# PSUM readers in a fixed order, a score buffer that outlives the attention, and a new order list, in a planned transformer block

## The chip, the cores and the metric

One core of one Trainium2 chip. The metric is the device time of one execution, in microseconds; the time before is the median of three runs. Engine names are those of the profile: PE is the matmul engine (PEld its weight loads), DVE the vector engine, ACT the activation engine, POOL the general engine, SP the engine whose queue issues nearly all DMAs.

## The reference

One block over x of 1 x 2048 x 512, float32: adaptive layer norm from a condition c, an attention of 32 heads of 16 with a compressive memory over four segments of 512, then a dense layer pair (512 to 1792 to 512) with squared ReLU. Cut to its core:

```python
mod = silu(c) @ w_mod                      # six rows of 512: sa, ca, ga, sb, cb, gb
h = layernorm(x) * (1 + ca) + sa
q, k, v = h @ wq, h @ wk, h @ wv           # 32 heads, 4 segments
for s in range(4):
    logits = q_s @ k_s.T * scale + mask    # mask: -1e9 where the key comes after the query
    a_dot = softmax(logits) @ v_s
    a_mem = (phi(q_s) @ M) / (phi(q_s) @ z + 1e-6)      # phi(t) = t + 1 or exp(t)
    o_s = g * a_mem + (1 - g) * a_dot
    M, z = M + phi(k_s).T @ v_s, z + phi(k_s).sum()
x = x + ga * (o @ wo)
h = layernorm(x) * (1 + cb) + sb
x = x + gb * (relu(h @ w1 + b1) ** 2 @ w2 + b2)
```

## The kernel before

**The work.** Matmuls run on float32 split into a high part (rounded to the engine's short float32) and a low part, three products for one. The attention goes in 16 units, u = 0 to 15: four segments s of four column blocks cc of 128 (eight heads each). A unit has a projection to q and k (`qk`), whose two PSUM banks are read by ACT (high part), DVE (low part), and for the memory by ACT twice more (Exp and Relu). The four parts lie in a tile `sg`; twelve DMAs per unit (line 847) spread them into `ST`, a buffer of 12 slots with one row per head set. `a_quad` computes scores for the row maxima (PE line 902, DVE line 907), which go through a transpose and a small DMA into ST's last row (`mt`, line 975). `b_quad` computes the scores again (line 1071), ACT takes the exponential (line 1088) into tiles `pt`, POOL masks the diagonal (line 1075), PE multiplies by v (line 1130), and after both halves a transpose (`fin`, line 1165) and DVE normalize. `mem` reads and updates the memory. Output rows of the first three segments go to DRAM (`o_dram`) and come back (`ot`) with rows of x (`xw`) for the product with wo (`wo_tile`, lines 1226 to 1228); the last segment's stay in `X1L`. `ln2` norms and transposes (`blnq`), ACT and DVE each apply two of four affines into `h2raw`.

**The dense layers.** The first product is done by a seven-product scheme for 2 x 2 blocks: `make_w1` forms seven blocks of w1 in DRAM (`w1_dram`) during the attention; `h2_ops` forms four differences T1 to T4 on POOL (line 1321) and seven operands H2o, each a high part by ACT and a low part by DVE (lines 1335, 1337); `ffn1` runs seven products (line 1484) per pair of column blocks p, `ffn2` the second layer (lines 1548 to 1550). w1 blocks come back by `fetch_w1` (line 1434, 1.75 MB each), w2 by `load_w2` (lines 1442 to 1446).

**The plan.** Nothing is issued where the code calls for it. Each step is a node of `Plan`, made by `op(engine, duration, function, priority, after=..., get=..., put=...)`: `after` are the nodes it waits for, `get` takes a slot of a pool, `put` gives slots back when their last user has run. `Plan.run` plays all nodes with assumed durations and latencies, with one running node per engine, and `emit` then issues the program in the order of the starts. Where `ORDER` has a list for an engine, that engine takes its nodes strictly in that order; a number is the node's place in the order of creation, and 8-39 stands for 8, 9, up to 39. PE has 1,315 entries, ACT 945, DVE 897, POOL 342, SP 403. The waits of the chip follow from the tiles that the issued instructions touch, not from the plan's edges.

Pools that matter here: `bank` (8 PSUM banks), `P` (3 tiles of 8 KB per partition, for `pt` and early weights), `sg` (1 tile of 8 KB), `g` (16 tiles of 2 KB), `w1` (2), `rr` (4), `tt` (3).

**Memory.** `ST` lies in the attention's pool `sb`. `open_ffn` closes that pool and opens `sb2`, in whose memory the dense layers' tiles are made. Its node `N_FFN` waits for all nodes made before it, the whole attention. These wait for `N_FFN`: the T differences, operands H2o 2 to 6, the w1 and w2 loads, and the four wo tiles of the last segment.

```python
N_FFN = op("NIL", 0.0, open_ffn, -20.0, after=list(PL.nodes))
```

## Time and profile before

| | us |
|---|---|
| median of the runs before | 773.69 (770.69 to 774.9) |
| the profiled execution, its own time | 773.55 |
| its span (first to last recorded instruction) | 771.7 |
| PE busy in the span | 755.8 |
| DVE, ACT, POOL busy | 595.1, 441.8, 321.6 |

How to read it: a row of the timeline has start, length, engine, line, operation and tiles. A row of the waits reads "engine line <- releaser: us in total, times, longest us", idle time of the engine by what ended it. The chain of waits is the work that ended last, followed back from the end. An issue on SP's queue (SPq) is not the transfer; that lands later. The attention fills the span up to about 450 us, the dense layers the rest.

### The profile page before, as it was taken

Reading aid. Unit: us, or ns where it says so; the run is one execution under the profiler, and the core shown is the slowest. Engines: PE = TensorE matmul, PEld = TensorE weight load, DVE = VectorE, ACT = ScalarE, POOL = GpSimd, SP = SyncE. Lnnn points to the kernel's source line nnn. Section 1 sums busy time; section 2 is a strip of 40 time slices with the busy share of each in tenths; the row PEclk is TensorE's granted clock in tenths of the full one; section 3 lists DMA queues with packets and bytes.
Section 4 is the critical chain, followed back from the end, with each engine's and each line's share of the span. In section 5 each row is a group of like instructions: output and inputs, shape, how many; then the busy total and the mean of one; then the engine's idle time right before and its main releaser. Section 6 shows DMA issues by size and latency. Waiting matters only on the chain.

```text
span 771.7 us, 18017 instructions
## 1 busy us (share of the span) xinstructions
PE 755.8 (98%) x6649; PEld 598.6 (78%) x6649; DVE 595.1 (77%) x1591; ACT 441.8 (57%) x1001; POOL 321.6 (42%) x400
## 2 busy tenths in 40 slices
PE   9999999999999999998999999999999999999998
PEld 8986667666787667775666678989889899989886
DVE  5887797889799697888899798777875875576554
ACT  2669878799979987786856754654211321231110
POOL 5574776578968677474313362441010020000000
PEclk9999999999999999999999999999999999999999
DMA  8686773445645334537560084865435555544641
GB/s 271 215 264 168 207 238 97 142 133 154 186 156 146 78 92 141 160 96 207 179 190 29 10 293 146 283 229 187 178 118 183 192 203 193 190 144 170 232 164 55
DMA packets 59265, 129.65 MB, mean 168 GB/s; under 512 B 8613, under 2 KB 23977, under 8 KB 55594
## 3 DMA queue, kind: packets, MB, share of 16 engines
q1 hardware_dynamic: 59026, 128.37, 51.8%
q8 instruction: 53, 0.87, 0.5%
q14 instruction: 34, 0.28, 0.1%
q10 hardware_dynamic: 152, 0.13, 0.1%
HBM read 81.29 MB, written 20.19 MB: 131 GB/s over the span
## 4 chain that ended last, share of the span: by engine, by line
PE 79%; ACT 6%; DVE 5%; DMA 4%; SPq 2%; issue 2%; POOL 0%; ACTq 0%; DVEq 0%; POOLq 0%
PE bh L1484 17%; PE bqk L795 8%; PE bpf L1549 7%; PE bpf L1548 7%; PE bpf L1550 7%; PE bpv L1130 6%; PE bv L868 5%; PE bpb L1071 5%; PE ba L902 5%; ACT pt L1088 3%; PE bwarm L542 2%; PE bwop L1226 2%; DVE ba L907 2%; PE blnq L613 2%; SPq L847 1%
## 5 line engine op out<-in xcount | busy, mean ns | idle before, releaser
L907 DVE CUSTOM_DVE_ANT_0 ba<-ba,msk 128x384 f32<-128x384 f32 (+2 forms) x384 | 192.6, 531 | 32.5 <-PE ba L902 23.3
L1088 ACT ACTIVATE pt<-bpb 128x512 f32<-128x512 f32 x320 | 170.3, 613 | 19.8 <-PE bpb L1071 18.1
L1484 PEld LDWEIGHTS bh<-H2o,w 128*128 128x128 f32 x1176 | 154.7, 189 | 11.2 <-ACT p L1510 1.3
L1484 PE MATMUL bh<-H2o,w 128*128 128x256 f32 x1176 | 158.2, 282 | 0.6 <-ACT p L1510 0.6
L1075 POOL TENSOR_SCALAR_AFFINE_SELECT pt<-pt 128x512 f32<-128x512 f32 x128 | 79.3, 636 | 99.7 <-ACT pt L1088 64.4
L795 PE MATMUL bqk<-HT,WQK 64*128 64x512 f32 x720 | 103.0, 397 | 0.0
L1530 ACT CAST rr<-xx 128x512 fp32r<-128x512 f32 x56 | 34.6, 621 | 97.7 <-DVE xx L1520 55.2
L1071 PE MATMUL bpb<-ST 64*128 64x256 f32 (+2 forms) x512 | 81.0, 351 | 5.4 <-DVE mx L907 3.0
L1130 PE MATMUL bpv<-pt,VT 128*32 128x512 f32 (+3 forms) x1024 | 82.6, 448 | 0.5 <-DVE mx L907 0.5
L902 PE MATMUL ba<-ST 63*128 63x256 f32 (+2 forms) x512 | 77.5, 344 | 1.8 <-DMA ST<-pad 0.8
L795 PEld LDWEIGHTS bqk<-HT,WQK 64*128 64x128 f32 x720 | 66.9, 185 | 10.9 <-issue 1.0
L902 PEld LDWEIGHTS ba<-ST 63*128 63x128 f32 x512 | 48.8, 185 | 27.4 <-issue 5.6
L1071 PEld LDWEIGHTS bpb<-ST 64*128 64x128 f32 x512 | 51.3, 186 | 23.3 <-DVE mx L907 6.0
L1548 PE MATMUL bpf<-w,rr 128*128 128x512 f32 x160 | 63.5, 397 | 0.0
L1549 PE MATMUL bpf<-w,rr 128*128 128x512 f32 x160 | 63.0, 394 | 0.0
L1550 PE MATMUL bpf<-w,rr 128*128 128x512 f32 x160 | 62.5, 391 | 0.0
L1130 PEld LDWEIGHTS bpv<-pt,VT 128*32 128x32 f32 x1024 | 28.4, 111 | 35.6 <-issue 26.0
L907 DVE DVE_READ_ACCUMULATOR2_ANT mx<- 128x1 f32 x384 | 54.3, 141 | 0.0
L868 PE MATMUL bv<-WVO,HT 64*128 64x512 f32 x384 | 54.2, 396 | 0.0
L1532 DVE TENSOR_TENSOR rr<-xx,rr 128x512 fp32r<-128x512 f32 x56 | 40.2, 720 | 15.3 <-ACT rr L1530 15.3
L1510 ACT COPY p<-bh 128x256 f32<-128x256 f32 x28 | 10.4, 370 | 60.2 <-PE bh L1484 41.2
L1321 POOL TENSOR_TENSOR tt<-tt,h2raw 128x512 f32<-128x512 f32 x4 | 5.2, 1296 | 91.1 <-DVE H2o L1337 91.1
(171 smaller groups left out, 1466.9 us busy)
## 6 DMA issues: line engine op xcount, KB each, us to landing
w<-w1d SPq DMA_DIRECT2D x28, 1792.0 KB
ST<-sg SPq DMA_DIRECT2D x192, 128.0 KB
w1d<-X1L SPq DMA_DIRECT2D x21, 512.0 KB
xt<-in_A_x SPq DMA_DIRECT2D x16, 256.0 KB
wm<-in_w_mod SPq DMA_DIRECT2D x16, 256.0 KB
xw<-in_A_x SPq DMA_DIRECT2D x16, 256.0 KB
X1L<-in_B_w SPq DMA_DIRECT2D x7, 512.0 KB
wr<-in_B_w SPq DMA_DIRECT2D x14, 256.0 KB
```

What stands on the lines that cost most here:

```text
L795: nc.tensor.matmul(bank(banks[w]), W3(w, k, x, cols.start, cols.stop)[r], HT[r, y, k], start=turn == k == i == 0, stop=turn == 1 and k == ...
L868: nc.tensor.matmul(bank(banks[t]), HT[r, x, k, (t2 + t) * P:(t2 + t + 1) * P], WVO[r, k, y], start=turn == k == i == 0, stop=turn == 1 and ...
L902: nc.tensor.matmul(dst[:, c0:c0 + n], ST[b:b + 63, 0, sl, qt * P:(qt + 1) * P], ST[b:b + 63, 1, sl, :n], start=True, stop=True)
L907: nc.vector.tensor_tensor_reduce(i, i, msk[:, 512 - n:], scale=1.0, scalar=-3e38, op0=ALU.add, op1=ALU.max, accum_out=o)
L1071: nc.tensor.matmul(dst, ST[b:b + 64, 1, sl, kb * P:(kb + 1) * P], ST[b:b + 64, 0, sl, q0:512], start=True, stop=True)
L1075: nc.gpsimd.affine_select(out=ap, in_=ap, pattern=[[0, ap.shape[1]], [1, P]], compare_op=ALU.is_ge, fill=0.0, base=0, channel_multiplier=-1)
L1088: ns = [op("ACT", 0.49, lambda j=j: nc.scalar.activation(buf("PPP"[n], pt)[:, i + j], bank(keys[j]), AF.Exp, scale=0.25), pr[slot] + 0.01 ...
L1130: nc.tensor.matmul(bank(o)[32 * hq:32 * hq + 32, q0:q0 + src.shape[1]], v[:, a:a + 32], src, start=start, stop=stop, tile_position=(0, 32 ...
L1484: nc.tensor.matmul(pb(i), A[:, x, kk], B[:, y, kk], start=kk == j == 0, stop=kk == 1 and j == 2)
L1548: nc.tensor.matmul(q, rh, wh, start=(i == 0), stop=False)
L1549: nc.tensor.matmul(q, rh, wl, start=False, stop=False)
L1550: nc.tensor.matmul(q, rl, wh, start=False, stop=(i == NF - 1))
```

## The change

Five things.

1. Readers of one PSUM bank get an order as plan edges: Exp and Relu of a qk bank wait for DVE's low part (before: for ACT's high part only); in `ln_transposed` and `ln2`, DVE's half of the affine waits for ACT's half. The operations are the same.
2. `sg` tiles are taken from pool `P`, which has 4 slots instead of 3; the separate `sg` pool of 1 is gone.
3. `ST` moves out of `sb` into a pool of its own that stays open. In the dense layers its slots are used again: 1 to 3 for `rr` tiles (the fourth in `sb2`), 4 to 7 for `w1` slot 0, 8 to 11 and 0 for operands H2o 2 to 6.
4. `h2_ops` of the first segment is made before `N_FFN` and no longer waits for it: its T differences take tiles of pool `g`, its operands wait for the last readers of the ST slots (units 14 and 15). The first w1 load waits for unit 13's readers. Node numbers from the old `N_FFN` (2777) to the old place of these 18 nodes (2883) go up by 18: the wo tiles' first transpose 2781 becomes 2799, the first w1 load 2820 becomes 2838.
5. All five lists of `ORDER` are new up to the last layers. Of the lists, the parts that matter in what follows: SP's four wo loads (2623, 2627, 2631, 2635), unit 14's fills (2392 to 2403) and the `ot` and `xw` loads (2640, 2650, 2660); PE's entries from the last wo matmul of the first three segments (2754 to 2757) through the first products (2903 to 2909) and the transposes of X1L (before: 2811, 2781, 2791, 2801; after: 2809, 2819, 2829, 2799); POOL's T differences (after: 2777 to 2780).

```diff
     "PE": """
...
-2611 2599 2716 2751 2717 2770 2615-2617 2766 2754 2619 2755-2757 2811 2781 2791 2801 2814-2816 2794 2817 2795
-2784-2785 2796 2906 2903-2904 2786 2905 2908 2797 2787 2804-2806 2907 2909 3142 2807 3066 3138 2926 2928 2927 3064
...
+2583 2566 2570 2495 2588 2747 2711 2592 2596 2603 2593 2599 2606 2611 2714-2717 2751 2594 2615-2617 2754 2619
+2755-2757 2903 2906 2904 2809 2819 2905 2908 2812 2822 2813 2823-2824 2829 2814 2799 2825 2832 2907 2802-2803 2909
...
     "POOL": """
...
+2428 2366 2531 2354 2513 2361-2362 2760 2462 2455 2463 2552 2467 2478 2485 2490 2486 2777-2778 2579 2780 2587 2586
+2779 2591 2609 2602 2610 2614 2885 2840 2844 3132 2849 2853 2862 2858 2867 2876 3389 2871 2894 2880 2889 3646
...
     "SP": """
...
-2110-2111 2115 1982 1793 269 2269 1460 2272 2278 2270 2277 2273 2003 2271 2275 276 2279 2268 2276 2274 2400 2176 2394
-2393 279 1928 2399 2398 2197 2392 2401 2396 2631 2397 2402 2623 2635 2403 2627 2395 2640 2650 2321 2660 2300 2670 2524
-2516-2518 2063 2710 2522 2520 2680 2525 2690 2519 2527 2523 2720 2700 2526 2521 2424 2750 2730 2445 2740 2548 2569
...
+1982 2115 2278 2275 2277 2268 1460 2270 2272 1658 2269 2271 276 2279 2273 2276 2003 2274 2176 2197 2400 2395 1928 1793
+2631 2627 2635 2623 2394 2640 2403 2399 2392 2398 2393 2321 2650 279 2397 2660 2401-2402 2300 2063 2516 2527 2518 2521
+2396 2524 2680 2523 2525 2517 2670 2700 2720 2520 2519 2740 2522 2730 2424 2526 2690 2445 2710 2838 2548 2569 2750
+2796-2797 2839 2843 2828 2798 2818 2884 2808 2847 2856 2848 2852 2861 2865 2857 2866 2874 2901 2875 2879 2870 2883
...
@@ -432,6 +431,9 @@
     gb_dram = dram.tile([1, D], F32, name="gb_dram")
     st_all = const.tile([P, NT, 2], F32, name="st_all")
     small = ctx.enter_context(tc.tile_pool(name="small", bufs=2))
+    NSLOT = 12
+    ST = ctx.enter_context(tc.tile_pool(name="stp", bufs=1)).tile([P, 2, NSLOT, 512], F32R, name="ST")
+    STf = ST.bitcast(F32)
     ph1 = ExitStack()
     sb = ph1.enter_context(tc.tile_pool(name="sb", bufs=1))
     ps = ctx.enter_context(tc.tile_pool(name="ps", bufs=1, space=PSUM))
@@ -450,10 +452,7 @@
                                 fill=0.0, base=-DH, channel_multiplier=1)
-    NSLOT = 12
     NV = 6
-    ST = sb.tile([P, 2, NSLOT, 512], F32R, name="ST")
-    STf = ST.bitcast(F32)
     VT = [sb.tile([P, 4 * VROW + 16], F32, name=f"VT{i}") for i in range(NV)]
     MB = sb.tile([P, 4, VROW], F32, name="MB")
     nc.gpsimd.memset(MB, 0.0)
@@ -461,11 +460,12 @@
         nc.gpsimd.memset(v, 1.0)
-    POOLS = {"bank": 8, **BANKS, "xr": 4, "P": 3, "g": 16, "sg": 1,
+    POOLS = {"bank": 8, **BANKS, "xr": 4, "P": 4, "g": 16,
              "mx": 2, "mt": 1, "oT": 2, "mv": 2, "ac": 1, "#F": 4, "xx": 3, "rr": 4, "wr": 3,
              "w1": 2, "w2": 5, "p1": 1, "u2": 2, "u3": 1, "tt": 3, "wx": 1, "wy": 1}
     HOME, KEPT = dict.fromkeys(("oraw", "e", "phi0", "phi1", "pk", "am", "on", "xr"), "g"), {}
+    HOME["sg"] = "P"
     PL = Plan(POOLS, ORDER)
     def op(*args, get=(), **kw):
@@ -635,7 +635,8 @@
             af = [op("ACT", 1.38, lambda: ln_affine("av", buf(pool, f), bank(b), sc, bi), pr + 0.01, after=[n, *MODC[sc]], put=[b])]
         else:
             af = [op("ACT", 0.69, lambda: ln_affine("a", buf(pool, f), bank(b), sc, bi), pr + 0.01, after=[n, *MODC[sc]], put=[b]),
-                  op("DVE", 0.64, lambda: ln_affine("v", buf(pool, f), bank(b), sc, bi), pr + 0.01, after=[n, *MODC[sc]], put=[b])]
+                  None]
+            af[1] = op("DVE", 0.64, lambda: ln_affine("v", buf(pool, f), bank(b), sc, bi), pr + 0.01, after=[af[0]], put=[b])
         h = act(512, lambda: ln_split(dst(), t, TL[f], low)[0](), pr + 0.02, sbuf=True, after=[*af, *wait], put=[f])
         l = op(low, 1.24 if low == "POOL" else 0.6, lambda: ln_split(dst(), t, TL[f], low)[1](), pr + 0.03, after=[h], put=[f], lock=True)
         return [h, l]
@@ -833,10 +834,10 @@
             ev[w] = (hi, lo)
             if s > 0 if w == 0 else s < NS - 1:
                 e, f = ("e", u, w), (f"phi{w}", u)
-                x1_ = act(512, lambda b=b, e=e: nc.scalar.activation(buf("e", e), bank(b), AF.Exp), p2 + 0.001, after=[hi],
+                x1_ = act(512, lambda b=b, e=e: nc.scalar.activation(buf("e", e), bank(b), AF.Exp), p2 + 0.001, after=[lo],
                           get=[("e", e)], put=[b])
                 x2_ = act(512, lambda b=b, f=f, w=w: nc.scalar.activation(buf(f"phi{w}", f), bank(b), AF.Relu), p2 + 0.002,
-                          after=[hi], get=[(f"phi{w}", f)], put=[b])
+                          after=[lo], get=[(f"phi{w}", f)], put=[b])
                 m_ = op("POOL", 1.57, lambda e=e: nc.gpsimd.tensor_scalar(TL[e], TL[e], 1.0, None, op0=ALU.min), p2 + 0.002, after=[x1_])
                 PHN[u, w] = op("POOL", 1.23, lambda e=e, f=f: nc.gpsimd.tensor_tensor(TL[f], TL[f], TL[e], op=ALU.add), p2 + 0.003,
                                after=[m_, x2_], put=[e])
@@ -1209,6 +1210,12 @@
     def x1(g):
         return LT["X1"][g // 4][:, g % 4]
+    def rr_tile(k):
+        if k not in TL:
+            q = PL.slot[k]
+            TL[k] = ST[:, :, 1 + q, :] if q < 3 else FF["sb"].tile([P, 2, L], F32R, name="rr", tag="rr3")
+        return TL[k]
+
     WON = []
     def load_wo(k, pr, after):
@@ -1253,8 +1260,10 @@
         n = pe("F", 0.355, tr, pr, after=heads + [N_FFN] if last else [ld], get=[("#D", b), (pool, ot)], put=() if last else [o])
         def hi():
-            home = FF["sb"] if last else LT["op"]
-            TL[ot] = home.tile([P, 2, D], F32R, name="oT", tag=f"{pool}{PL.slot[ot]}")
+            if last:
+                rr_tile(ot)
+            else:
+                TL[ot] = LT["op"].tile([P, 2, D], F32R, name="oT", tag=f"oT{PL.slot[ot]}")
             nc.scalar.copy(TL[ot][:, 0], bank(b))
         h = act(512, hi, pr + 0.01, after=[n], put=[b])
         l = dve(512, lambda: nc.vector.tensor_tensor(TL[ot][:, 1], bank(b), TL[ot][:, 0].bitcast(F32), op=ALU.subtract), pr + 0.01,
@@ -1292,8 +1301,9 @@
             def both(k, affine=affine):
                 affine(k)
                 affine(k + 1)
-            RAW[s] += [op(e, c, lambda k=k, both=both: both(k), pr[t] + 0.01, after=[n, *MODC[CB], *RAWUSE[s - 1], N_LATE], put=[b])
-                       for e, c, k in (("ACT", 0.69, 0), ("DVE", 0.64, 2))]
+            for e, c, k in (("ACT", 0.69, 0), ("DVE", 0.64, 2)):
+                n = op(e, c, lambda k=k, both=both: both(k), pr[t] + 0.01, after=[n, *MODC[CB], *RAWUSE[s - 1], N_LATE], put=[b])
+                RAW[s].append(n)
@@ -1303,9 +1313,7 @@
     def operand(j):
         if j < 2:
             return LT["ops"][j]
-        if "opb" not in FF:
-            FF["opb"] = [FF["sb"].tile([P, 2, 2, HALF], F32R, name=f"H2o{i + 2}") for i in range(5)]
-        return FF["opb"][j - 2]
+        return ST[:, :, (8, 9, 10, 11, 0)[j - 2], :].rearrange("p h (k n) -> p h k n", k=2)
     def h2_ops(s, at):
@@ -1317,10 +1325,13 @@
             key = ("tt", s, name)
             def go():
-                TL[key] = FF["sb"].tile([P, 2, HALF], F32, name="tt", tag=f"tt{PL.slot[key]}")
+                if s:
+                    TL[key] = FF["sb"].tile([P, 2, HALF], F32, name="tt", tag=f"tt{PL.slot[key]}")
+                else:
+                    TL[key] = sb.tile(SHAPES["e"], F32, name="tt", tag=f"g{PL.slot[key]}").rearrange("p (k n) -> p k n", k=2)
                 nc.gpsimd.tensor_tensor(TL[key], blk[x](), blk[y](), op=ALU.subtract)
-            node[name] = op("POOL", 1.55, go, at[0] + 0.09 * k, after=[N_FFN, *RAW[s], *(node[q] for q in (x, y) if q in node)], get=[("tt", key)],
-                            put=[("tt", s, q) for q in (x, y) if q in node])
+            node[name] = op("POOL", 1.55, go, at[0] + 0.09 * k, after=[*RAW[s], *(node[q] for q in (x, y) if q in node), *([N_FFN] if s else [])],
+                            get=[("tt" if s else "g", key)], put=[("tt", s, q) for q in (x, y) if q in node])
             blk[name] = lambda: TL[key]
         t_of("T1", "B12", "B11", 0)
         t_of("T2", "B22", "T1", 1)
@@ -1331,7 +1342,7 @@
         for j, name in enumerate(BO):
             key = ("tt", s, name)
             put = [key] if name in node else []
-            wait = [N_LATE if j < 2 else N_FFN] + (OPUSE[s - 1, name] if s else [])
+            wait = OPUSE[s - 1, name] if s else [N_LATE] if j < 2 else [q for pp in range(4) for q in STU[4 * (NU - 1 if j == 6 else NU - 2) + pp]]
             h = act(512, lambda j=j, name=name: nc.scalar.copy(operand(j)[:, 0], blk[name]()), at[1 + j], sbuf=True,
                     after=[*([node[name]] if name in node else RAW[s]), *wait], put=put)
             l = op("DVE", 0.6, lambda j=j, name=name: nc.vector.tensor_tensor(operand(j)[:, 1], blk[name](), operand(j)[:, 0].bitcast(F32),
@@ -1340,6 +1351,7 @@
             if name not in node:
                 use += [h, l]
         RAWUSE[s] = use
+        return [q for name in BO if name not in node for q in OPN[s][name]]
     gb = lambda: buf("oraw", ("t", "gb"))
     for p in range(NF // 2):
@@ -1398,14 +1410,14 @@
         FF["gbb"] = sb2.tile([P, D], F32, name="gbb")
         FF["b2g"] = sb2.tile([P, D], F32, name="b2g")
-    N_FFN = op("NIL", 0.0, open_ffn, -20.0, after=list(PL.nodes))
+    z = e + K_FF
+    def us(t):
+        return z + t / 14.0
+    free_of = {n.seq for n in h2_ops(0, [us(-7 + 0.7 * j) for j in range(8)])}
+    N_FFN = op("NIL", 0.0, open_ffn, -20.0, after=[n for n in PL.nodes if n.seq not in free_of])
     del HOME["xr"]
-    z = e + K_FF
     n_gbb = sp(lambda: nc.sync.dma_start(FF["gbb"], gb_dram.to_broadcast([P, D])), z - 3, 1 << 18, after=[N_FFN])
     n_b1 = sp(lambda: nc.sync.dma_start(b1c, b1.rearrange("(f p) -> p f", p=P)), z - 2.8, 1 << 14, after=[N_FFN])
-    def us(t):
-        return z + t / 14.0
-
     NP = NF // 2
     STEP = 10.44
     W1N, W2N = {}, {}
@@ -1417,6 +1429,8 @@
     def w1slot(p, s):
         k = ("w1", p, s)
+        if PL.slot[k] == 0:
+            return ST[:, :, 4:8, :].rearrange("p h s n -> p h (s n)")[:, :, :7 * 2 * P].rearrange("p h (a k n) -> p h a k n", a=7, k=2)
         if k not in TL:
             TL[k] = FF["sb"].tile([P, 2, 7, 2, P], F32R, name="w1", tag=f"w1{PL.slot[k]}")
         return TL[k]
@@ -1431,7 +1445,11 @@
     def fetch_w1(p, s, t0):
         key = ("w1", p, s)
-        n = sp(lambda: nc.sync.dma_start(w1slot(p, s).bitcast(F32), w1_dram[p]), us(t0 - 12), 7 << 18, after=[N_FFN, *W1D[p]], get=[("w1", key)])
+        first = p == s == 0
+        n = sp(lambda: nc.sync.dma_start(w1slot(p, s).bitcast(F32), w1_dram[p]), us(t0 - 12), 7 << 18, get=[("w1", key)],
+               after=[*W1D[p], *([q for pp in range(4) for q in STU[4 * (NU - 3) + pp]] if first else [N_FFN])],
+               soft=() if first else [LT["w1"]])
+        LT["w1"] = n
         W1N[p, s] = dict.fromkeys(AO, [n])
     def load_w2(p, t0):
@@ -1453,7 +1471,6 @@
     for p in range(NP):
         fetch_w1(p, 0, STEP * p)
         load_w2(p, STEP * p)
-    h2_ops(0, [us(-7 + 0.7 * j) for j in range(8)])
     kb = ("b2b",)
     n = sp(lambda: nc.sync.dma_start(buf("xr", kb), bass.AP(tensor=b2.tensor, offset=b2.offset, ap=[[0, P], [1, D]])), z + 0.2, 1 << 18,
            get=[("xr", kb)], after=[X1N[4 * NS - 1]])
@@ -1507,7 +1524,7 @@
             return op("DVE", D_ + 0.06, lambda: nc.vector.scalar_tensor_tensor(dst(), pb(i), bias[j], other(), op0=ALU.add, op1=ALU.add),
                       us(t0 + t), after=[N[i], n_b1, *after], **kw)
         L_, R_ = [lambda i=i: X[i]()[:, :HALF] for i in (0, 1)], [lambda i=i: X[i]()[:, HALF:] for i in (0, 1)]
-        a1 = act(HALF, lambda: nc.scalar.copy(P1(), pb(1)), us(t0 + 0.9), after=[N[1]], get=[("p1", p1)], put=[K[1]])
+        a1 = act(HALF, lambda: nc.scalar.copy(P1(), pb(1)), us(t0 + 0.9), after=[N[1], N_FFN], get=[("p1", p1)], put=[K[1]])
         d2 = add(1.7, U2, 6, P1, [a1], get=[("u2", u2)], put=[K[6]])
         d3 = add_b(2.4, U3, 7, U2, 1, [d2], get=[("u3", u3)], put=[K[7]])
         d4 = add_b(4.4, U2, 5, U2, 0, [d2, d3], put=[K[5]])
@@ -1524,9 +1541,7 @@
                 n = act(512, lambda i=i: nc.scalar.activation(X[i](), X[i](), AF.Square), us(t0 + t), sbuf=True, after=[n])
             def rr_(i=i):
-                if rr[i] not in TL:
-                    TL[rr[i]] = FF["sb"].tile([P, 2, L], F32R, name="rr", tag=f"rr{PL.slot[rr[i]]}")
-                return TL[rr[i]]
+                return rr_tile(rr[i])
             h = act(512, lambda i=i, rr_=rr_: nc.scalar.copy(rr_()[:, 0], X[i]()), us(t0 + t + 0.7), sbuf=True, after=[n], get=[("rr", rr[i])],
                     put=[x_[i]])
             l = op("DVE", 0.6, lambda i=i, rr_=rr_: nc.vector.tensor_tensor(rr_()[:, 1], X[i](), rr_()[:, 0].bitcast(F32), op=ALU.subtract),
```

293 lines of the change are left out of this document (143 added, 150 removed), and 11 rows, old and new, of the table ORDER.

## The prediction

> **What bounds the kernel now.** First view: the head of the profile page, the busy time of the engines.
>
> ```profile
> span 771.7 us, 18017 instructions
> PE 755.8 (98%) x6649; PEld 598.6 (78%) x6649; DVE 595.1 (77%) x1591; ACT 441.8 (57%) x1001; POOL 321.6 (42%) x400
> ```
>
> PE is busy for 98% of the span; no other engine passes 78%. So the question is where the 771.7 - 755.8 = 15.9 us without a matmul lie. The second view, busy time by stage, answers it (columns: stretch, its length, then busy time and count of PE, PEld, DVE, ACT, POOL, then clock, DMA share, GB/s).
>
> ```profile
> 0.00:25.00 25.00, 23.10 (x182) 21.41 (x183) 13.98 (x30) 9.50 (x20) 10.91 (x31) 1.00 0.85 279
> 25.00:350.00 325.00, 318.86 (x3642) 230.71 (x3642) 274.02 (x882) 271.84 (x656) 233.76 (x287) 0.99 0.53 154
> 350.00:375.00 25.00, 22.83 (x239) 13.61 (x236) 21.48 (x65) 19.38 (x43) 8.67 (x14) 0.93 0.64 191
> 375.00:450.00 75.00, 75.00 (x628) 50.99 (x627) 65.11 (x187) 48.51 (x103) 23.05 (x34) 1.00 0.37 119
> 450.00:475.00 25.00, 23.80 (x143) 20.29 (x142) 22.18 (x38) 10.91 (x22) 11.47 (x10) 1.00 0.55 186
> 475.00:768.00 293.00, 292.25 (x1825) 261.62 (x1823) 197.68 (x393) 81.61 (x161) 33.77 (x27) 1.00 0.52 184
> 768.00:771.70 3.70, 0.00 (x0) 0.00 (x0) 0.62 (x1) 0.00 (x0) 0.00 (x0) 0.96 0.20 74
> ```
>
> The gaps: 1.9 us at the start and 3.7 at the end, which nothing in the diff touches; 6.1 in the attention up to 350; 2.2 between 350 and 375; none up to 450; 1.2 at the change to the dense layers; 0.75 in the dense layers' 293 us. The dense layers have nothing to give. What can be won lies in 25 to 475.
>
> A gap in this count is too small, though. The third view, the timeline of PE where the attention ends, shows why (columns: start, length, engine, line, operation, tiles; in brackets the idle time before it and what ended it).
>
> ```profile
> 451.20 0.49 PE L1252 MATMUL bwot<-ident,X1L 128*128 128x128 f32 x3
> 452.49 1.64 PE L1252 MATMUL bwot<-ident,X1L 128*128 128x128 f32 x13 [0.80 <-DVE X1L L1188]
> 454.20 0.40 PE L1227 MATMUL bwop<-WVO,oT 128*128 128x512 f32 x1
> 454.92 0.50 PE L1228 MATMUL bwop<-WVO,oT 128*128 128x512 f32 x1 [0.32 <-DVE oT L1260]
> 455.25 0.39 PE L1226 MATMUL bwop<-WVO,oT 128*128 128x512 f32 x1
> 455.48 0.40 PE L1227 MATMUL bwop<-WVO,oT 128*128 128x512 f32 x1
> ```
>
> Back to back, a matmul of 512 columns starts 455.48 - 455.25 = 0.23 us after the one before, but its row is 0.39 long. Each gap hides 0.16 us under the end of the row before it. By starts, the wait for X1L costs 452.49 - 451.20 less three steps of 0.113 (13 transposes in 1.64 with a last row of some 0.28) = 0.95 us, and the wait for oT 454.92 - 454.20 - 0.23 = 0.49.
>
> **The change part by part.** The counts of the order text first: PE's list holds 1,315 entries and 160 changes of array mode in both versions, so no work and no mode change is added or removed. What moves is waiting.
>
> *Part 1, the dense layers begin earlier.* ST outlives the attention, so the first w1 block (into ST slots 4 to 7, after unit 13), the seven H2o operands and the T subtractions no longer wait for open_ffn. In the new PE list three products (2903, 2906, 2904) stand between the last wo matmul (2757) and the first transpose of X1L, and two more after the second transpose; before, four transposes stood there at once.
>
> ```profile
> 442.45 0.33 SPq L1434 DMA_DIRECT2D w<-w1d  x1
> 449.36 2.53 POOL L1321 TENSOR_TENSOR tt<-h2raw 128x512 f32<-128x512 f32 x2 [4.12 <-DVE h2raw L1290]
> 451.04 1.39 DVE L1188 TENSOR_TENSOR X1L<-X1L,am 128x512 f32<-128x512 f32 x1
> 451.96 1.61 POOL L1321 TENSOR_TENSOR tt<-h2raw,tt 128x512 f32<-128x512 f32 x1
> 457.17 2.58 DVE L1337 TENSOR_TENSOR H2o<-tt,H2o 128x512 fp32r<-128x512 f32 x2
> 457.46 3.45 POOL L1443 TENSOR_TENSOR wr<-wr,gbb 128x512 f32<-128x512 f32 x2
> 459.68 1.78 DVE L1337 TENSOR_TENSOR H2o<-h2raw,H2o 128x512 fp32r<-128x512 f32 x1
> 460.85 2.25 PE L1484 MATMUL bh<-H2o,w 128*128 128x256 f32 x18
> 461.38 0.68 DVE L1337 TENSOR_TENSOR H2o<-tt,H2o 128x512 fp32r<-128x512 f32 x1
> ```
>
> Today the first product starts at 460.85, because T1 starts at 449.36 and the operands follow. Three products are 18 matmuls, 2.1 us by starts, and cover the 0.95 and most of the 0.49; the rest of the 475 window's idle time (0.1 here and there) I leave. Taken: -1.4 us; ends 0 (the operands come as late as the transposes do now) and -2.0 (all idle time of 450 to 475 by starts). If the operands are late, the cover is gone and PE stands before 2903 instead of before the transpose. The four T subtractions (2.53 + 1.61 + one more of 1.3) go between the last unit's selects on POOL; POOL is busy 23 of 75 us there, so they cost nothing unless a select meets one, 1.3 us at most, with three score groups queued on PE as cover.
>
> Beside that the H2o rows: one takes 0.68 alone and 1.78 at 459.68 while POOL's L1443 runs, as the X1L add at 451.04 takes 1.39 beside a T subtraction. If all seven, moved into the attention's tail, met POOL like that, DVE would need 7 x 1.1 = 7.7 us more of the 9.9 us it has idle in 375 to 450, so nothing on PE as long as they fall into idle time. The Trainium skill ("SBUF — State Buffer", Who interferes with whom) says that a DVE instruction with two SBUF inputs contends with a GpSimd instruction that reads SBUF; the row agrees, and by it this part of the change would be a loss on DVE and not a gain, by up to those 7.7 us.
>
> *Part 2, the order.* One stall in the trace is long and has a place. The chain of waits and the waits of PE and DVE show it.
>
> ```profile
> 356.89 2.95 DMA wo<-in_A_wo
> 358.85 1.09 SPq L1216 DMA_DIRECT2D wo<-in_A_wo  x2
> 359.86 0.79 DVE wo L1217
> 361.37 0.50 PE bpb L1071 x3
> PE bpb L1071 <- DVE mx L907: 3.0, 4, 2.1
> DVE wo L1217 <- DMA wo<-in_A_wo: 2.8, 2, 2.1
> L847 SPq DMA_DIRECT2D ST<-sg x192: 607/608/2007, 32.4 to 395.8; - x192
> 362.25 0.58 SPq L1241 DMA_DIRECT2D ot<-o_dram  x1
> 362.88 0.56 SPq L1242 DMA_DIRECT2D xw<-in_A_x  x1
> 366.27 1.41 SPq L975 DMA_DIRECT2D ST<-mt  x2
> ```
>
> SP issues a wo load at 356.89, it lands 2.95 us later, DVE stands 2.1 us before L1217 with the row maxima (L907) behind it, and PE stands 2.1 us before a score group. In the old SP list eight of unit 14's twelve fills (L847, 0.61 us of SP each) stand ahead of that load (2631); in the new one two do, and the four wo loads follow each other. Six fills less are 3.6 us, more than the 2.1 that the load was late. Taken: -2.0. The price is on the other side of the queue. All fills of unit 14's first half (2392 to 2394, 2398 to 2400) stood ahead of the wo loads; its last one (2393) now stands behind the four of them (1.09 for two), one pair of ot and xw loads (0.58 + 0.56) and two more fills: 2.2 + 1.1 + 1.2 = 4.5 us. PE hides that only if these scores come late enough in its list; taken at 0, ends -2.1 and +2.4.
>
> For all else that is rearranged between 25 and 450 no row of before can say what it brings. The nearest are the gaps left, 6.1 us visible up to 350, and the single stalls of 2.1. I take 0, ends -4 (two thirds of the visible gaps) and +4 (two stalls like 361.37).
>
> *Part 3, the readers.* Exp and Relu of a qk bank now follow DVE's subtraction of the low part, DVE's half of an affine follows ACT's. In the waits of ACT, DVE and PE:
>
> ```profile
> ACT e L836 <- DVE sg L831: 3.3, 6, 0.8
> DVE sg L831 <- ACT phi L838: 1.6, 4, 0.7
> DVE h2raw L1290 <- ACT h2raw L1288: 5.9, 5, 2.6
> ACT lnf L619 <- DVE lnf L621: 2.1, 1, 2.1
> PEld ba L902 <- ACT e L836: 1.6, 2, 1.1
> PE ba L902 <- ACT phi L838: 0.4, 1, 0.4
> ```
>
> These engines already wait for each other, 12.9 us in all, with no edge between them in the old plan: as these rows show, readers of one bank are put in sequence anyway, in the order in which the plan had them start. So the edges add no wait on the chip; they only let the order be chosen with it. What reached PE is 0.4 visible and 1.6 on the weight loads. Taken: -0.8; ends -2.0 and +1.0 (Exp always last makes phi later; phi is needed by L995 and L1020 alone). Beside this the eight-KB tiles are four of one pool instead of three and one: PE waits for a pt tile's exp in nothing over 0.4, so 0, ends -1 and +1.
>
> **Sum.** The profiled execution took 773.55 us, span and 1.85 around it, 0.14 under the median 773.69. 773.55 - 1.4 - 2.0 - 0.8 = 769.35; 769.3 us, 0.57% less. Differences under some 0.5%, 3.9 us, are about what a measurement of this kernel can't tell from no change; the bound is 769.8.
>
> **Rivals.**
> A. *Given back* (no change). The stalls above go, but PE meets the next late thing: the attention is bounded by DVE and ACT as much as by PE in places (274 and 272 of 325 us busy up to 350), and a group that starts 2 us earlier waits 2 us longer for its exp. Then only the transition stays: 773.55 - 1.4 = 772.2. For it: the 6.1 us are spread thin. Against it: 350 to 450 has idle time on both.
> B. *Unit 14 starved* (slower). SP's queue from 345 on: the first half's fills come 4.5 us later, and the second half's last one (2396) stands behind two more ot pairs, two mt stores (1.41 each) and four fills of unit 15, another 2.3 + 2.8 + 2.4 = 7.5 us; the scores of unit 14 wait, and behind them DVE, ACT and the wo products. PE then stands 4.5 to 12.0 us; against the 4.2 won elsewhere it decides from 4.2 on. With half of the 7.5: 769.35 + 4.5 + 3.75 = 777.6. Against it: PE is without a gap from 375 to 450, so work is queued there.
> C. *More room than the rows of PE show.* Hidden gaps of 0.16 each mean that a better order can win more than 15.9 - 5.6. With -4 in the attention and the far ends of parts 1 to 3 (-2.0, -2.1, -2.0, -1): 762.4. The Trainium skill ("Perfetto Trace Analysis", Identifying the Most-Contended Engine) holds matmul busy time to be no measure of how near PE is to its limit, and takes weight-load busy time. By it the attention (25 to 450: 295.3 of 425, 69%) is far from the dense layers (261.6 of 293, 89%) and at their share would need 331 us, an estimate from the stages' rows that would put the time at 680; the mode changes, the same 160 in both lists, and the short products speak against reading it so, and no run here shows it.
>
> **How the numbers follow.** Forecast (765.5 to 770.5): 0.44, of which 0.38 is under 769.8. A (770 to 775): 0.31, same. B (774 to 781): 0.13, of which 0.07 is over 777.5. C (758 to 765.5): 0.12, faster. So faster 0.50, same 0.43, slower 0.07; I move 0.04 from same to slower, since the whole list between 25 and 450 is new and may hold a stall with no row before: 0.50, 0.39, 0.11. The range 761.5 to 777.5 leaves out the far half of C and the upper half of B, with what was moved to it: 2 in 10 at most. The likeliest case's own range is 765.5 to 770.5.
>
> **What would show it.** Part 1: in the changed profile the first bh product (L1484's line) starts near 451, right behind the last wo matmul of the attention, instead of 460.85, before the transposes of X1L, and PE's gap with releaser X1L is gone. Part 2: no wait of PE for mx near 2 us between 350 and 375; DVE's wait for a wo load is 0; if B is right, PE or PEld waits for ST filled from sg there. Part 3: ACT's wait for sg grows or stays, and DVE's for phi is gone. The dense layers' rows stay at 293 us from 475 on. The prediction is wrong if PE's idle time in 25 to 350 differs from 6.1 us by more than 4, or if the transition shows PE standing for H2o.

## The result and the profile after

| | before | after |
|---|---|---|
| median, us (4 runs each) | 772.19 (770.51 to 774.90) | 762.53 (761.64 to 765.40) |
| ratio | | 0.9857, 95% interval 0.9821 to 0.9893 |
| profiled execution, us | 773.55 | 762.98 |
| its span, us | 771.7 | 761.3 |

The change makes the kernel 1.4% faster, where 0.57% was forecast. The engines' busy times and the stages of the changed kernel (columns as before):

```profile
PE 749.7 (98%) x6649; PEld 598.1 (79%) x6649; DVE 582.7 (77%) x1591; ACT 440.1 (58%) x1001; POOL 322.3 (42%) x400
```

```profile
25.00:350.00 325.00, 319.64 (x3646) 233.61 (x3644) 271.55 (x895) 271.23 (x658) 234.68 (x286) 0.99 0.53 149
350.00:375.00 25.00, 24.60 (x269) 15.11 (x266) 23.86 (x67) 21.93 (x46) 12.14 (x20) 1.00 0.79 239
450.00:475.00 25.00, 25.00 (x157) 22.18 (x156) 18.95 (x34) 12.02 (x23) 9.97 (x8) 1.00 0.59 220
475.00:757.50 282.50, 282.39 (x1764) 253.34 (x1762) 186.27 (x380) 74.81 (x149) 30.36 (x24) 1.00 0.50 179
```

PE's share is 98% again. The transition has lost its gaps (25.00 of 25, 23.80 before), and the last stage is 282.5 us long instead of 293. But by these rows almost nothing happened up to 350 us: PE idle 5.4 us instead of 6.1. That is misleading, because equal times are not equal work. A mark that stands for the same step in both kernels shows it: the transposes that close a unit's head outputs (bfin), 16 for each unit. PE's timeline of before, the rows of units 5, 8, 10, 11 and 12, then the last matmul:

```profile
209.59 0.66 PE L1165 MATMUL bfin<-ident,oraw 64*128 64x64 f32 x16
286.66 0.66 PE L1165 MATMUL bfin<-ident,oraw 64*128 64x64 f32 x16
337.75 0.66 PE L1165 MATMUL bfin<-ident,oraw 64*128 64x64 f32 x16
361.66 0.94 PE L1165 MATMUL bfin<-ident,oraw 64*128 64x64 f32 x14
383.71 0.66 PE L1165 MATMUL bfin<-ident,oraw 64*128 64x64 f32 x16
767.49 0.40 PE L1550 MATMUL bpf<-w,rr 128*128 128x512 f32 x1
```

The same of after:

```profile
209.12 0.66 PE L1166 MATMUL bfin<-ident,oraw 64*128 64x64 f32 x16
286.24 0.71 PE L1166 MATMUL bfin<-ident,oraw 64*128 64x64 f32 x16
334.36 0.65 PE L1166 MATMUL bfin<-ident,oraw 64*128 64x64 f32 x16
356.15 0.65 PE L1166 MATMUL bfin<-ident,oraw 64*128 64x64 f32 x14
377.37 0.66 PE L1166 MATMUL bfin<-ident,oraw 64*128 64x64 f32 x16
444.47 0.39 PE L1235 MATMUL bwop<-WVO,oT 128*128 128x512 f32 x1
444.70 0.85 PE L1501 MATMUL bh<-H2o,ST 128*128 128x256 f32 x6
756.99 0.40 PE L1565 MATMUL bpf<-w,ST 128*128 128x512 f32 x1
```

The lead is 0.5 us at unit 5 and 0.4 at unit 8: the first half of the attention shows next to no gain. It is 3.4 at unit 10, 5.5 at unit 11, 6.3 at unit 12, 6.5 where the last wo product of the first three segments ends (451.20 and 444.70), and 10.5 at the last matmul. So the attention's units 8 to 12 bring 5.9, its last units 0.2, and the change to the dense layers and these 4.0. (What else stands ahead of a mark differs by an entry or two between the lists, so a single mark may be off by some work.)

For the experiments I use a yardstick that needs no common mark: the kernel's planner has a fixed duration for each of PE's 1,315 entries and for each mode change. The time in the trace between two points of equal sum, less that sum, is what PE lost in that stretch, hidden gaps included. It is worked out from all matmul starts of a trace. In us, by stretch of that sum (in brackets the time in before at which it begins):

| profile | 0 to 60 (2) | 60 to 240 (67) | 240 to 300 (263) | 300 to 340 (329) | 340 to 480 (375) | 480 to 720 (519) | sum |
|---|---|---|---|---|---|---|---|
| before | 5.1 | 16.3 | 6.2 | 5.7 | 3.7 | 2.7 | 39.6 |
| after | 4.8 | 16.9 | 2.8 | 2.1 | 1.7 | 0.8 | 29.1 |

Before lost 39.6 us by this count, two and a half times the 15.9 that its busy rows show. The gain is 3.4 + 3.6 in the second half of the attention, 1.9 at the transition, 1.9 in the dense layers, and nothing in the first half.

Not all of these 39.6 us are waits: the yardstick also counts time at a low clock. The clock record of every profile has windows of 3.41 us at full clock (PEclk 1.00) or at half (0.50), called half windows below. Two rows of before, the window with the stall at 359 us and the one behind it, then eight pv products of 512 columns in that half window and, from after, eight at full clock:

```profile
358.38:361.79 3.41, 1.34 (x12) 0.90 (x13) 1.93 (x4) 1.95 (x4) 0.63 (x1) 1.00 0.90 264
361.79:365.21 3.42, 3.42 (x34) 1.53 (x30) 2.61 (x10) 2.79 (x5) 1.86 (x3) 0.50 0.85 262
363.25 1.93 PE L1130 MATMUL bpv<-pt,VT 128*32 128x512 f32 x8
431.11 1.06 PE L1131 MATMUL bpv<-pt,VT 128*32 128x512 f32 x8
```

The 19 profiles of this case hold 37 half windows between 10 and 750 us; the yardstick finds 1.2 to 2.1 us in each, 1.5 on average. Before has two, at 81.9 (in the column 60 to 240) and at 361.8 (in 300 to 340); after has two in a row at 169.9 (in 60 to 240). So the sums of the two can be compared as they are, but not these columns. Less 1.5 for each half window, up to 240 before has 19.9 and after 18.7, a gain of 1.2 and not nothing, and in 300 to 340 4.2 and 2.1, a gain of 2.1 and not 3.6.

Between 263 and 300 us before has eight gaps of 0.26 to 1.0 us by starts, 4.0 in all, four of them before a pv product, one before the transposes of phi. In PE's waits of before in that window only 1.0 us of it has a row:

```profile
PE bpb L1071 <- DMA ST<-mt: 0.6, 1, 0.6
PE bat L967 <- ACT e L836: 0.2, 1, 0.2
PE bpkt L1020 <- ACT pt L1088: 0.2, 1, 0.2
```

Over the same work after has one gap above 0.25, of 0.39.

### The profile page after: what moved, and what is told of

It reads as the page before. It is cut to its first block, busy times and chain, and to the rows that moved or that the text cites. A ratio compares the mean times of both kernels' runs of the same rounds, so it can differ in the third digit from the quotient of the medians.

```text
span 761.3 us, 18032 instructions
## 1 busy us (share of the span) xinstructions
PE 749.7 (98%) x6649; PEld 598.1 (79%) x6649; DVE 582.7 (77%) x1591; ACT 440.1 (58%) x1001; POOL 322.3 (42%) x400
## 4 chain that ended last, share of the span: by engine, by line
PE 86%; ACT 4%; DMA 3%; SPq 2%; POOL 2%; issue 2%; DVE 1%; ACTq 0%; POOLq 0%; DVEq 0%
PE bh L1501 18%; PE bpv L1131 8%; PE bqk L796 7%; PE bpf L1564 7%; PE bpf L1563 7%; PE bpf L1565 7%; PE bpb L1072 5%; PE ba L903 5%; PE bv L869 5%; PE bwop L1233 2%; PE bwarm L542 2%; DMA w1d<-X1L 2%; PE bwop L1235 2%; PE bwop L1234 2%; PE blnq L613 2%
## 5 line engine op out<-in xcount | busy, mean ns | idle before, releaser
L1089 ACT ACTIVATE pt<-bpb 128x512 f32<-128x512 f32 x320 | 172.4, 621 | 18.4 <-PE bpb L1072 15.8
L1072 PE MATMUL bpb<-ST 64*128 64x256 f32 (+2 forms) x512 | 78.5, 351 | 1.7 <-DVE mx L908 1.2
L796 PEld LDWEIGHTS bqk<-HT,WQK 64*128 64x128 f32 x720 | 68.8, 185 | 10.7 <-DVE mx L908 1.2
L903 PE MATMUL ba<-ST 63*128 63x256 f32 (+2 forms) x512 | 75.1, 346 | 1.5 <-ACT pt L1089 0.7
L1332 POOL TENSOR_TENSOR tt<-h2raw 128x512 f32<-128x512 f32 x8 | 10.9, 1367 | 142.6 <-ACT h2raw L1297 98.6
L1527 ACT COPY p<-bh 128x256 f32<-128x256 f32 x28 | 10.4, 371 | 93.1 <-PE bh L1501 64.9
L1501 PEld LDWEIGHTS bh<-ST,w 128*128 128x128 f32 x420 | 56.5, 189 | 3.5
L1501 PE MATMUL bh<-ST,w 128*128 128x256 f32 x420 | 59.0, 282 | 0.0
L1501 PE MATMUL bh<-ST 128*128 128x256 f32 x420 | 58.4, 282 | 0.0
L1501 PEld LDWEIGHTS bh<-ST 128*128 128x128 f32 x420 | 55.8, 190 | 3.1
L1563 PE MATMUL bpf<-w,ST 128*128 128x512 f32 x136 | 53.8, 395 | 0.0
L1545 ACT CAST ST<-xx 128x512 fp32r<-128x512 f32 x43 | 26.1, 619 | 47.6 <-DVE xx L1537 19.1
L1564 PE MATMUL bpf<-w,ST 128*128 128x512 f32 x136 | 53.6, 394 | 0.0
```

Source lines behind the costliest of these rows:

```text
L796: nc.tensor.matmul(bank(banks[w]), W3(w, k, x, cols.start, cols.stop)[r], HT[r, y, k], start=turn == k == i == 0, stop=turn == 1 and k == ...
L903: nc.tensor.matmul(dst[:, c0:c0 + n], ST[b:b + 63, 0, sl, qt * P:(qt + 1) * P], ST[b:b + 63, 1, sl, :n], start=True, stop=True)
L1072: nc.tensor.matmul(dst, ST[b:b + 64, 1, sl, kb * P:(kb + 1) * P], ST[b:b + 64, 0, sl, q0:512], start=True, stop=True)
L1089: ns = [op("ACT", 0.49, lambda j=j: nc.scalar.activation(buf("PPP"[n], pt)[:, i + j], bank(keys[j]), AF.Exp, scale=0.25), pr[slot] + 0.01 ...
L1501: nc.tensor.matmul(pb(i), A[:, x, kk], B[:, y, kk], start=kk == j == 0, stop=kk == 1 and j == 2)
L1563: nc.tensor.matmul(q, rh, wh, start=(i == 0), stop=False)
```

## Experiments

Theory L, as I went in: the gain is in the lists. The old ones were made for readers of one bank that run side by side; on the chip these take turns, and the lists that know it wait less. Rivals: the edges themselves (E); gains that are given back later (G); gains that add up by place (P). Beside each kernel before ran on the same chip (medians 772.9 to 774.2).

**Edges alone, lists alone.** e1 is before with this edit only, e2 the changed kernel with all reader edges undone (here the reverse of the first pair of lines, and the halves of both affines independent again):

```diff
-  x1_ = act(512, ... AF.Exp), p2 + 0.001, after=[hi], ...
-  x2_ = act(512, ... AF.Relu), p2 + 0.002, after=[hi], ...
+  x1_ = act(512, ... AF.Exp), p2 + 0.001, after=[lo], ...
+  x2_ = act(512, ... AF.Relu), p2 + 0.002, after=[lo], ...
```

> The kernel before with its own five order lists, and only the edges for Exp and Relu of a q/k bank added (they follow DVE's low part instead of the copy by ACT); memory, dense layers and lists as before. Theory L (the lists): an edge by itself brings nothing, what is gained lies in lists that were searched with the edge known; with the old lists Exp and Relu now stand in ACT's queue until DVE has come to its subtraction, so 770 to 780 us, not below 770 (before: 772.2). Rival E (the edges themselves): that the low part goes first brings the score operands earlier by an Exp and a Relu, 0.6 us each; then at least half of the 6.5 us that the attention won is there with the old lists: 765 to 769 us.

> The changed kernel with its own new lists, memory and dense layers, and only the reader edges taken out again (Exp and Relu after the copy; the halves of the two affines independent of each other), so that what the plan starts first on a bank goes first. Theory L: the lists alone carry the gain, 761 to 765 us, ACT's wait for sg and DVE's wait for phi differ from the changed kernel's by 2 us or less. Rival E: without the edges at least half of the attention's 6.5 us is lost, 766 to 770 us.

> The changed kernel once more, unchanged, to stand beside the others of this call and beside e2 (764.4 us, the same without the reader edges): 761 to 765 us. If the edges matter with the new lists, it is more than 1.5 us under e2 in ratio to before; if they don't, the intervals of the two lie in each other.

> e2 again (the changed kernel without the reader edges), for the 2 us between it and the changed kernel, beside which it stands here on one chip. If the edges bring something with the new lists, 764 to 765 us and ratios apart; if e2 was spread, 762 to 763.5 us.

> The changed kernel, for the comparison with e11: 761.5 to 763.5 us.

e1: 781.73 us, ratio 1.0112 (1.0087 to 1.0138). The edges of Exp and Relu, with the old lists, cost 9 us, more than the 770 to 780 us expected (the edges of the affines were not run alone). E falls, and so does the prediction's sentence that edges add no wait on the chip: they turn the turn-taking round. ACT's waits of e1 between 25 and 450 us:

```profile
ACT e L836 <- DVE sg L831: 10.2, 9, 1.5
ACT phi L838 <- DVE sg L831: 5.0, 4, 2.0
```

15.2 us of waiting for DVE's low part, against 3.3 for ACT and 1.6 for DVE in before. In its yardstick 8.4 us more stand in the stretch 60 to 240. It has four half windows there and before one, which makes 4.5 of the 8.4: in this profile about half of the price is waiting, and half the clock. In after these waits are as good as gone, though the edges are there:

```profile
ACT e L837 <- DVE sg L832: 0.6, 1, 0.6
DVE sg L832 <- ACT sg L830: 9.5, 6, 5.0
DVE h2raw L1299 <- ACT h2raw L1297: 1.9, 3, 1.5
```

The new lists have DVE waiting for ACT's copy (9.5 us, 2.4 before) and not ACT for DVE: the low part is taken at once, and ACT has other work before the Exp. The second affine's wait fell from 5.9 to 1.9.

e2 and e11, the same kernel in two sessions: 764.44 and 765.01 us, ratios 0.9888 (0.9861 to 0.9915) and 0.9889 (0.9866 to 0.9912). e8 and e12, the changed kernel beside others: 762.39 and 763.18, ratios 0.9859 (0.9842 to 0.9876) and 0.9872 (0.9846 to 0.9899). So the lists, with the new pools and the new memory that e2 keeps, carry four fifths of the gain without any edge. The means of ten runs each are 764.6 and 762.9; the 1.7 us between them have a 95% interval, by resampling these runs, of 0.6 to 2.7. The intervals of the ratios still overlap, so an own gain of the edges is likely and small.

**Which stretch of the lists.** The next kernels have the changed code without reader edges, and lists put together from the two versions by planned time (numbers from 2777 on translated, since the dense layers' nodes moved):

```diff
  for e in engines:
+     head = [n for n in OLD[e] if planned_old[n] < T]
+     ORDER[e] = head + [n for n in NEW[e] if n not in head]
```

T is 420, 345, 300, 245 and 146 us of the old plan for e3, e4, e17, e13 and e7. e5 has the new list for the first 125 us, then the old one up to 420, then the new; e6 is new but for 125 to 245.

> The changed kernel's code and memory without the reader edges; the five lists are those of before up to some 430 us of the run, and the new ones for what is left (the change to the dense layers and these). By place, at equal work done, the trace of after is 6.5 us ahead of before's where the wo products of the first three segments end, and 10.4 at the end. If the places add up, this kernel gains only the 3.9 us that come after: 768 to 769 us. Rival G (given back): an earlier start of the dense layers is lost again at their weights, 771 to 773 us. Rival O (the two parts hang together): the tail brings over 6 us with an attention that is late: under 766.

> As the kernel before it, but the new lists begin some 65 us earlier, before the four wo loads of the attention's last quarter, so that the stretch with the wait for the wo load (356.9 to 361.4 in before) is ordered anew, and nothing earlier. At equal work after is 2.9 us ahead there before the stretch and 6.6 behind it, so by places 3.7 us more than the tail alone: 764 to 766 us. Rival G: the wait goes and the next late thing takes its place, 768 to 769 us as with the tail alone. DVE's wait for a wo load should be 0 in both cases.

> As e13, the new lists from some 310 us. At equal work the stretch of unit 8, 263 to 288 us of before, costs 2.1 us less with the new lists in every profile, and it stays old here; the stretch with the wo loads is new. S: some 2 us above e13 and some 3 under e4, 766 to 767.5 us. W: as e4, 768 to 770 us.

> As e4, the lists of before at first and the new ones after, without the reader edges, but the new ones begin some 255 us into the run instead of 355. e5 to e7 say that the new lists of the first 255 us bring nothing that stays. If so (S, the second half of the attention), this kernel is at the level of e2, e6 and e7: 764 to 766 us. Rival W (the lists only win as a whole): it stays with e4, 768 to 770 us.

> The changed kernel without the reader edges, the lists of before up to some 155 us of the run and its own new ones from there. By places (P): after's lead of 4.4 us at that point is gone and the middle's loss stays, 766 to 769 us. Given back (G): the lead was lost again by 240 us anyway, so without it nothing is lost, 762 to 765 us.

> As e3 (new memory, no reader edges, new lists from some 430 us on), with the new lists also for the first 130 us; between them the lists of before. At equal work after is 3.6 us ahead of before's at 130 us. By places (P): 3.6 us less than e3, 766 to 767.5 us. Given back (G): what the start wins is lost by whatever follows it, since the middle is bound by DVE and ACT: 769 to 771 us as e3.

> The changed kernel without the reader edges, its new lists everywhere but in the middle, some 130 to 255 us of the run, where the order of before stands. In that stretch after loses 4.4 us against before at equal work. By places (P): the old middle is the better one and this kernel beats the changed one, 758 to 760 us. Given back (G): the middle's loss comes of the start's gain, whichever list stands there, 762 to 765 us. Reader waits (L): the old middle has Exp and low part of one bank side by side, and its waits come back, 765 to 768 us; then ACT's wait for sg and DVE's for phi show 2 us or more in the middle.

| kernel: where the list is new | median | ratio (95%) | 60 to 240 | 240 to 300 | 300 to 340 | 340 to 480 | 480 to 720 | half windows, 60 to 240 and 300 to 340 | mean, less the clock |
|---|---|---|---|---|---|---|---|---|---|
| e3: from 420 | 770.24 | 0.9967 (0.9942 to 0.9991) | 15.8 | 4.6 | 4.9 | 2.7 | 1.8 | 1, 0 | 765.9 |
| e4: from 345 | 769.31 | 0.9947 (0.9927 to 0.9967) | 18.8 | 5.2 | 3.3 | 1.8 | 0.8 | 3, 0 | 765.6 |
| e17: from 300 | 768.74 | 0.9940 (0.9919 to 0.9961) | 17.2 | 6.7 | 2.1 | 2.0 | 0.8 | 2, 0 | 765.7 |
| e13: from 245 | 767.74 | 0.9929 (0.9903 to 0.9955) | 19.9 | 2.7 | 2.8 | 2.1 | 0.8 | 4, 0 | 762.5 |
| e7: from 146 | 764.93 | 0.9907 (0.9872 to 0.9942) | 15.7 | 2.8 | 2.6 | 1.8 | 0.8 | 1, 0 | 762.9 |
| e6: all but 125 to 245 | 764.60 | 0.9885 (0.9861 to 0.9909) | 16.3 | 2.7 | 2.1 | 2.5 | 0.8 | 0, 0 | 762.4 |
| e5: to 125 and from 420 | 771.48 | 0.9960 (0.9941 to 0.9979) | 17.9 | 4.9 | 7.1 | 2.7 | 0.8 | 1, 2 | 767.5 |
| e2: everywhere | 764.44 | 0.9888 (0.9861 to 0.9915) | 15.9 | 2.8 | 2.1 | 1.7 | 0.8 | 0, 0 | 763.4 |

The last column is an estimate: the mean of all runs, less 1.5 us for each half window that their mean granted clock stands for, with standard errors of 0.4 to 1.2. By it before (77 runs) is at 769.5 and the changed kernel (14 runs) at 761.1.

The columns from 240 on are clean: wherever the list is new, 240 to 300 costs 2.7 to 2.8 us instead of 4.6 to 6.7, and 300 to 340 2.1 to 2.8 (3.3 where it begins inside) instead of 4.9 to 7.1 (4.1 to 4.9 without the half windows). The new pools do not do this: e17 has them too, and differs from e13 only by the list that stands from 245 to 300, 6.7 against 2.7. The tail alone gives 0.3%, a little under the 4 us expected (P). A new start gives nothing that stays (e5 beside e3), and the old middle (e6) is no better than the new. The lead of 4.4 us that after has near 155 us, by the yardstick, is lost by 240 us; some 3 us of that are its two half windows, but e2, which has none, loses a lead of 3.0 as well, as G said.

By their medians three expectations of this group failed: e4 and e17 came out where the rivals had put them (769.3 and 768.7, not 764 to 766 and 766 to 767.5), and e13, expected at 764 to 766, at 767.7, while e7, with the new middle too, is at 764.9. In the profiles a large part of this is the clock. The four kernels with the same lists up to 240 us (e3, e4, e17, e13) range from 15.8 to 19.9 in that column, and from 13.9 to 14.3 without their half windows; e7 has 14.2. So e13's profile shows no wait that e7's lacks there, only three more half windows. By the last column the places come out: the tail gives 3.6 us, the list of 245 to 300 another 3.2, that of 300 to 420 nothing clear of the error (in the columns some 2 us), and e13 stands with e2, e6 and e7. What is not shown is whether the old middle behind an old start is what brings the half windows, or chance: all four runs of e13 have a clock of 0.990 to 0.995, the six of e7 0.993 to 0.998.

**The reader conflict taken away.** e9 is before, lists and all, with Exp and Relu reading ACT's copy, so that the bank has no third and fourth reader; e16 does it in e3, e14 in the changed kernel (phi is that of the rounded value in all three):

```diff
-  ... nc.scalar.activation(buf("e", e), bank(b), AF.Exp) ... put=[b])
+  ... nc.scalar.activation(buf("e", e), TL[sg].bitcast(F32)[:, 2 * w], AF.Exp) ... put=[sg])
```

> The kernel before, lists and all, with one thing taken away: Exp and Relu of a q/k bank read ACT's rounded copy in SBUF and not the bank, so that DVE's subtraction of the low part is the bank's only other reader and neither waits for the other (phi is then that of the rounded value). Theory R: the order between readers of one bank, which the old lists didn't have, is what before's attention loses, so ACT's wait for sg (3.3 us) and DVE's for phi (1.6) fall to 0 and 3 to 6 us of PE's idle time go: 766 to 770 us. Rival O: these waits lie beside other work, and the new lists win by other things than the readers: 771.5 to 773.5 us.

> e3 (the old attention, the new memory and the new lists from 430 us on) with Exp and Relu reading ACT's copy as in e9 (phi is then that of the rounded value). If what the readers cost and what the new tail brings are two things (A), they add: 770.2 - 4.5 = 765 to 767 us. If e9's gain was of the tail's kind, or only shifts work that waits elsewhere (G): 768 to 770 us.

> The changed kernel with Exp and Relu reading ACT's rounded copy in SBUF and not the bank, as e9 does for the kernel before (phi is then that of the rounded value; they follow the copy and not DVE's low part). If the new lists have taken in what the readers of one bank cost (R), taking that conflict away brings nothing more, 762 to 764 us, where it brought 4.5 us with the old lists. If the conflict still costs in them (C): 758 to 761 us, a version better than both. A copy held until the Exp is through keeps one of the four 8 KB tiles longer: if that decides (H), 765 to 768 us.

e9: 769.44 us, ratio 0.9939 (0.9914 to 0.9964). With the old lists the conflict cost 4.5 us, as theory R had it; ACT's wait for DVE's sg and DVE's for phi have no row left. (Its profiled execution was its slowest, 773.4 us, so its stretches aren't compared.) e16: 767.22, 0.9913 (0.9880 to 0.9946); the gains of e3 and e9 would add to 0.9906, so the two are different things and add (A). Together they are 0.9 of the 1.4%. e14: 766.01, 0.9905 (0.9875 to 0.9935), 3 us slower than the changed kernel. In the new lists the conflict costs nothing any more, and its removal brings nothing; that the 8 KB tile is held longer (H) fits the number, but no wait in the trace names it, so it isn't shown. No version here beats the changed kernel.

**Two single waits.** e10 moves the four wo loads together in before's SP list; e15 moves ACT's copy p ahead of one rr cast at two places of before's dense layers.

```diff
  "SP" (e10)
- ... 2392 2401 2396 2631 2397 2402 2623 2635 2403 2627 2395 ...
+ ... 2392 2631 2623 2635 2627 2401 2396 2397 2402 2403 2395 ...
  "ACT" (e15)
- 3190 3202 ... 3193 3223
+ 3202 3190 ... 3223 3193
```

> The kernel before with one edit in SP's list: the four wo loads stand together where the first of them would be due, ahead of four of unit 14's fills. Part 2 of the prediction: DVE's wait for a wo load goes from 2.8 us to 0, PE's 2.4 us stand near 361 goes, and nothing takes its place: 769.5 to 771 us. Rival G (next late thing): the maxima come in time, but PE then waits for an exp or a mask row a little later: 772 to 773 us. Rival B: the fills that now come 2 us later starve the scores of unit 14: over 773.5 us.

> The kernel before with two places of ACT's list changed, both in the dense layers: the copy of a product's half (p, L1510) stands ahead of one rr cast instead of behind it. Before's profile has PE waiting for p 0.6 us in two gaps, near 546 and 557 us, 1.0 us by starts; after's has none there. If ACT's list is the cause: both waits gone, 1.0 us less in the dense layers' stretch of the profile, and 772 to 773 us beside 773.4, which the runs hardly tell apart. If the cause is a late product or the rr slots: the gaps stay, or move to the second product behind.

e10: 772.78 us, ratio 0.9996 (0.9977 to 1.0015), not the 769.5 to 771 expected but G's 772 to 773. In its profile the stall did shrink, with no new one behind it: the stretch 300 to 340 went from 5.7 to 3.6 us. Of these 2.1 us, 1.5 are the half window that follows the stall in before and is missing here. Its waits there, and the stage row:

```profile
DVE wo L1217 <- DMA wo<-in_A_wo: 0.9, 1, 0.9
PE bpb L1071 <- DVE mx L907: 0.8, 1, 0.8
```

```profile
350.00:375.00 25.00, 24.10 (x242) 14.80 (x240) 23.22 (x74) 21.25 (x45) 9.93 (x16) 1.00 0.64 196
```

PE's wait for mx went from 2.1 to 0.8. Over the runs at most 1.8 us of it are left (the lower end of the interval). e15: 774.24, 1.0019 (0.9997 to 1.0040), above the 772 to 773 expected. PE's wait for p has no row left in its profile, but the dense layers' stretch fell by nothing (2.7): what PE gained at 546 us it lost before the next products, in pieces of 0.2 to 0.3. In the dense layers a single swap is given back. There the whole order differs, and the memory of the operand, w1 and rr tiles as well; no run has the one without the other, so which of them gives the 1.9 us isn't shown.

## Why the prediction was wrong

*Part 1* was right in mechanism. The first product starts at 444.70, right behind the last wo product, and PE's waits for X1L and oT have no row. By the yardstick the transition (340 to 480) gave 1.9, near the end of its range, against 1.4 taken. The price named beside it did not fall due: the add into X1L takes 0.68 us now (1.39 before), two H2o subtractions from tt 1.29 together (2.58; most of the operands lie in ST now):

```profile
440.32 0.68 DVE L1189 TENSOR_TENSOR X1L<-X1L,am 128x512 f32<-128x512 f32 x1
440.92 1.29 DVE L1348 TENSOR_TENSOR ST<-tt,ST 128x512 fp32r<-128x512 f32 x2
450.83 2.77 DVE L1348 TENSOR_TENSOR ST<-h2raw,ST 128x512 fp32r<-128x512 f32 x2
```

The rule of the Trainium skill ("SBUF — State Buffer", Who interferes with whom) is borne out by the last row, two subtractions of some 1.4 us each while POOL works on `wr` (450.06 to 454.75), but this part of the change was no loss.

*"The dense layers have nothing to give"* was wrong by 1.9 us. Their busy rows showed 0.75 idle in 293; by starts 2.7 stood there, and 0.8 stand now.

*Part 2*'s -2.0 was the right size for the stall: DVE waits for no wo load any more, PE's wait for mx is 1.2 us in two pieces over the whole attention, and the row of 350 to 375 is 24.60 with the clock at 1.00. The isolated edit kept 0 to 1.8 of it. *All else that is rearranged: 0* is the step that failed. The stretch 263 to 329 us, where no long wait was to be seen and the clock is full in both profiles, gave 3.4, and the one with the wo loads 3.6, of which e10's profile gives 2.1 to the loads (1.5 of them the half window behind the stall, a price that the prediction has nowhere): 4.9 us for a term taken as 0, past its own end of -4. That the 3.4 are the lists' work is shown by e13 beside e17 (2.7 against 6.7), and by e2 and e7. The cause of the miss lies in the measure: I bounded this term by the gaps that the busy rows leave, 6.1 us, having just shown that each gap hides 0.16 us; eight gaps of 263 to 300 us, 4.0 by starts, had 1.0 in rows.

*Part 3* was wrong in its reason. Readers do take turns in the order of the plan, as it said, but an edge changes that order, and with lists not made for it the price is 9 us (e1). What the old lists paid was not the 2.0 us that reached PE in rows, but 4.5 (e9). DVE's wait for phi is gone, as said; "ACT's wait for sg grows or stays" was the wrong way round: 3.3 fell to 0.6.

*Sum.* Forecast -1.4 - 2.0 - 0.8 = -4.2; found, by yardstick, -1.9 at the transition, -1.9 in the dense layers, -7.0 between 263 and 375 us and +0.3 before, -10.5 (-10.4 by the spans). Of the rivals C came true, with its time (762.4) and its mechanism, hidden gaps; that the time fits so closely is luck, since the 1.9 of the dense layers is in none of its terms. A was right for single edits and nearly for the first half of the attention. B didn't happen: no row has PE waiting for unit 14's fills. The test "PE's idle time in 25 to 350 differs by more than 4" could not have told: it moved by 0.7, while 3.4 us of lead were won by unit 10.

What stays open: why the old middle (146 to 245) behind an old start goes with more half windows; what the memory gives in the dense layers without the list; and whether a search without the edges would have found lists as good, since only their outcome could be run, not the search.

## What to carry to other kernels

Where PE's rows are longer than its step, bound what a new order can win by starts against a yardstick of durations (here 39.6 us), not by the idle time between rows (15.9), and take the time at half clock out before you compare two stretches: here it made equal waits look like 15.8 and 19.9 us. Where the scheduler of a kernel's order leaves out that readers of one bank take turns, its lists pay on the chip; give it the rule, but then search again, for the rule with the old lists cost twice what the conflict did. A stall that has a name in the waits is worth what remains after the next one, and an edit for it alone may be worth nothing.
